# Re-ordering the loads, the start and the last row tile of a squared-ReLU MLP kernel

## The chip, the cores and the metric

The kernel runs on one core of a Trainium2 chip. The metric is device time in microseconds (us). Each profile belongs to one execution; each timing is a set of executions, compared with executions of the kernel before in the same rounds on the same chip.

The span in a profile is shorter than the timed figure of the same execution by 1.8 us (kernel before).

PE is TensorE (matmuls and transposes), ACT is ScalarE, DVE is VectorE, POOL is GpSimd, SP is SyncE, which only issues DMAs here (`nc.sync`). PE writes its results to PSUM; copying them from there to SBUF is called *evacuation*. A load *lands* when all its data has arrived. In a profile line, out<-in are the tiles written and read, L192 is a line of the kernel, xN a count, and [0.42 <-DVE xTw L132] means that the engine was idle for 0.42 us before, until DVE's line 132 had written xTw.

## The reference

```python
B, S, D, F = 1, 2048, 576, 4608          # all bf16
def reference(x, w1, b1, w2, b2):
    h = jnp.einsum("bsd,df->bsf", x, w1) + b1
    r = jnp.where(h > 0, h, 0)
    h = r * r
    return jnp.einsum("bsf,fd->bsd", h, w2) + b2
```

## The kernel before

The sequence is worked in four blocks of 512 rows. For each block, the *first product* (18 steps j) makes h transposed from w1 and x transposed; ACT applies bias and ReLU, DVE squares into hT. The *second product* (four row tiles of 128 rows) multiplies hT by w2. x has to be transposed on TensorE (PE): all of block 0 before anything else, the next block's rows inside the second product of the block before it ("mid transposes").

w1 is kept as two halves on partitions 0-63 and 64-127, which two 64-row matmuls read side by side; so x transposed is kept in windows shifted by 64. For block 0 all ten windows are transposed on PE (40 transposes for four row tiles); for blocks 1 to 3 only every second window is (20 transposes a block), and the others are copied from those by DMA.

```python
    load_x_block(0, (nc.sync, nc.scalar))      # two DMAs of 288 KB
    # ... 8 warm-up matmuls on zeros, identity ...
    nc.scalar.dma_start(out=b1_rows[0:NFT, :], in_=b1.rearrange("(ft p) -> ft p", p=P))
    nc.scalar.dma_start(out=b2_bc[:], in_=b2.partition_broadcast(P))
    j_chunks = [(0, 1), (1, 2), (2, 4), (4, 8), (8, 12), (12, 16), (16, 18)]
    for ci, (j0, j1) in enumerate(j_chunks):   # two DMAs (halves) per piece of w1
        ...
    load_x_block(1, (nc.sync, nc.sync))
    for c in range(NFT // W2CH):               # six pieces of w2, 864 KB each
        nc.sync.dma_start(out=w2_sb[:, c*W2CH:(c+1)*W2CH, :], in_=...)
    # PE: transpose b1_rows, then the 40 transposes of x block 0
    ...
    def phase_b(sb, hT, mid_tile=None):        # second product
        for jj in range(RT):
            for i, ft in enumerate(ft_order):  # ft_order = 0, 18, 1, 19, 2, 20, ...
                if mid_tile is not None and i == NFT // 2:
                    mid_tile(jj)               # mid transposes, in jj = 0 and 1
                for h in range(2):
                    nc.tensor.matmul(po[h][:, 0:DH], lhsT=hT[:, ft, ...], rhs=w2_sb[:, ft, ...], ...)
            for h in range(2):
                nc.vector.tensor_tensor(out=o_sb[...], in0=po[h][...], in1=b2_f[...], op=ALU.add)
            nc.sync.dma_start(out=out2[...], in_=o_sb[:])
```

The order of use in the second product: its second step (i = 1) reads ft 18, which lies in the fourth piece of w2, and i = 24 and i = 25 read the third and the sixth piece.

## Time and profile before

| | us |
|---|---|
| time, median of 13 runs (300.46 to 301.67) | 301.05 |
| span of the profiled execution (itself timed 301.67, the slowest of these 13) | 299.9 |
| first product of block 0 starts / lasts | 9.19 / 37.0 |
| first product of blocks 1 to 3 | 35.08 each |
| first matmul of the first second product to the start of the last matmul | 249.9 |
| end of the last matmul to the end of the span | 3.5 |

The page's part on the chain that ended last, followed back from the last instruction, by engine and then by line (shares of the span):

```profile
PE 92%; DMA 6%; SPq 0%; DVE 0%; DVEq 0%; issue 0%
PE po L192 47%; PE ph L171 35%; PE ph L173 10%; DMA w_h<-in_w_dram 6%; PE tp L143 1%; SPq L98 0%; DVE o_sb L201 0%; SPq L66 0%; DVEq L251 0%
```

PE is the bottleneck; nearly all that is not PE is a wait for w1 (named w_h). The same chain in order of time (start in us, length in us, what):

```profile
1.23 6.12 DMA w_h<-in_w_dram
...
8.01 10.81 DMA w_h<-in_w_dram
18.86 0.39 PE ph L173
...
46.23 4.52 PE po L192 x36
50.75 0.56 PE tp L143 x10
...
296.25 0.46 DVE o_sb L201
```

The chain hangs on w1 until 18.82 us, 9.6 us after the first product began; from 46.2 us on it is matmuls without a break. PE's own waits (engine, line, what it waited for: total us, times, longest):

```profile
PE ph L173 <- DMA w_h<-in_w_dram: 1.5, 1, 1.5
PE b1T_ps L156 <- DMA b_rows<-in_b_dram: 1.5, 1, 1.5
PE wps L79 <- DVE wz L75: 1.3, 1, 1.3
PE ph L171 <- DVE xTw L132: 0.4, 1, 0.4
```

So PE is held twice: once by the b1 rows ahead of the x transposes, once by a w1 piece inside the first product. The timeline of the two ends (start, length, engine, line, operation, out<-in, count):

```profile
1.25 3.58 PE L79 MATMUL wps<-wz 128*128 128x512 bf16 x8 [1.25 <-DVE wz L75]
6.37 2.39 PE L122 MATMUL tp<-ident,x_sb 128*128 128x128 bf16 x40
...
9.19 0.37 PE L171 MATMUL ph<-xTw,w_h 64*128 64x512 bf16 x1 [0.42 <-DVE xTw L132]
...
296.25 0.82 DVE L201 TENSOR_TENSOR o_sb<-po,b_f 128x288 bf16<-128x288 f32 x2 [8.00 <-PE po L192]
297.10 0.33 SPq L207 DMA_DIRECT2D out_dram<-o_sb  x1
```

### The profile page before, as it was taken

The page shows a single profiled execution, that of the slowest core. Times are in us where ns is not written, and L with a number is a line of the kernel's source. Part 1 is how long each engine was busy: PE and PEld are TensorE (multiplying, and loading weights), DVE is VectorE, ACT ScalarE, POOL GpSimd, SP SyncE. Part 2 cuts the span into 40 slices and gives each one's busy share as a digit, 9 for nine tenths or more (in the row PEclk, how much of TensorE's full clock was granted, in tenths as well). Part 3 has the DMA queues.
Part 4 walks back from the last instruction along what each step waited for, and adds up shares of the span by engine and source line. Part 5 has one row for each costly group of instructions (what it writes and reads, how often), then busy time and mean ns, then how long its engine had stood idle before and what let it go on. Part 6 is the DMA issues. An engine that isn't in the chain of part 4 may idle for free.

```text
span 299.9 us, 5764 instructions
## 1 busy us (share of the span) xinstructions
PE 291.6 (97%) x2557; PEld 182.6 (61%) x2557; DVE 77.0 (26%) x183; ACT 102.9 (34%) x162; POOL 3.0 (1%) x16
## 2 busy tenths in 40 slices
PE   6979999999999999999999999999999999999995
PEld 2534447787744445887764444778774444477773
DVE  1434442111034444001114444211003444400111
ACT  2656663010056666110016666401004666600000
POOL 2000000000000000000000000000000000000000
PEclk9999999999999999999999999999999999999999
DMA  7999996240000000212000000022000000000000
GB/s 179 201 203 207 320 357 214 61 138 2 21 22 0 2 0 2 39 30 50 22 20 2 1 2 0 2 61 42 20 20 22 0 2 0 2 0 23 20 23 20
DMA packets 21337, 17.63 MB, mean 59 GB/s; under 512 B 3264, under 2 KB 21312, under 8 KB 21312
## 3 DMA queue, kind: packets, MB, share of 16 engines
q1 hardware_dynamic: 20256, 16.67, 22.8%
q10 hardware_dynamic: 1056, 0.60, 0.8%
q8 instruction: 20, 0.33, 0.5%
q14 instruction: 5, 0.04, 0.0%
HBM read 13.13 MB, written 2.36 MB: 52 GB/s over the span
## 4 chain that ended last, share of the span: by engine, by line
PE 92%; DMA 6%; SPq 0%; DVE 0%; DVEq 0%; issue 0%
PE po L192 47%; PE ph L171 35%; PE ph L173 10%; DMA w_h<-in_w_dram 6%; PE tp L143 1%; SPq L98 0%; DVE o_sb L201 0%; SPq L66 0%; DVEq L251 0%
## 5 line engine op out<-in xcount | busy, mean ns | idle before, releaser
L192 PE MATMUL po<-w_sb,hT 128*128 128x288 bf16 x1152 | 142.8, 286 | 0.0
L173 PE MATMUL ph<-xTw,w_h 64*128 64x512 bf16 x648 | 140.7, 376 | 1.5 <-DMA w_h<-in_w_dram 1.5
L171 PE MATMUL ph<-xTw,w_h 64*128 64x512 bf16 x648 | 140.7, 376 | 0.4 <-DVE xTw L132 0.4
L177 ACT ACTIVATE r<-ph,b1T 128x512 bf16<-128x512 f32 x144 | 91.2, 684 | 118.6 <-PE ph L173 107.5
L192 PEld LDWEIGHTS <-hT 128*128 128x128 bf16 x1152 | 112.1, 98 | 29.6 <-DVE hT L178 1.7
L171 PEld LDWEIGHTS <-w_h 64*128 64x128 bf16 x648 | 60.6, 94 | 61.0 <-issue 0.7
L178 DVE TENSOR_TENSOR hT<-r 128x512 bf16<-128x512 bf16 x144 | 61.3, 426 | 85.6 <-ACT r L177 85.0
L173 PEld LDWEIGHTS <-w_h 64*128 64x128 bf16 x648 | 60.4, 94 | 17.3 <-DMA w_h<-in_w_dram 2.4
L201 DVE TENSOR_TENSOR o_sb<-po,b_f 128x288 bf16<-128x288 f32 x32 | 13.2, 453 | 127.9 <-PE po L192 127.9
L145 ACT COPY xTw<-tp 128x640 bf16<-128x640 bf16 x12 | 7.7, 695 | 35.1 <-PE tp L143 35.1
L79 PE MATMUL wps<-wz 128*128 128x512 bf16 x8 | 3.6, 627 | 1.3 <-DVE wz L75 1.3
L143 PE MATMUL tp<-ident,x_sb 128*128 128x128 bf16 x60 | 4.3, 219 | 0.0
L143 PEld LDWEIGHTS <-x_sb 128*128 128x128 bf16 x60 | 3.9, 98 | 0.3
L130 ACT COPY xTw<-tp 128x640 bf16<-128x640 bf16 x4 | 2.5, 706 | 4.4 <-PE tp L122 4.4
L79 PEld LDWEIGHTS <-wz 128*128 128x128 bf16 x8 | 1.0, 138 | 2.9 <-issue 1.7
L122 PE MATMUL tp<-ident,x_sb 128*128 128x128 bf16 x40 | 2.4, 219 | 0.0
L122 PEld LDWEIGHTS <-x_sb 128*128 128x128 bf16 x40 | 2.3, 98 | 0.0
L160 DVE CAST b_f<-b_bc 128x576 f32<-128x576 bf16 x1 | 0.5, 460 | 5.8 <-DMA b_bc<-in_b_dram 5.8
L62 POOL MEMSET x_sb<- 128x256 bf16 x4 | 1.2, 312 | 58.1 <-PE tp L143 51.4
L85 ACT ACT_TABLE_LOAD x1 | 1.3, 1283 | 1.3 <-PEq L240 1.3
L132 DVE COPY xTw<-tp 128x640 bf16<-128x640 bf16 x4 | 1.7, 481 | 0.0
L156 PE MATMUL b1T_ps<-ident,b_rows 128*128 128x128 bf16 x1 | 0.2, 216 | 1.5 <-DMA b_rows<-in_b_dram 1.5
(13 smaller groups left out, 3.3 us busy)
## 6 DMA issues: line engine op xcount, KB each, us to landing
w_sb<-in_w_dram SPq DMA_DIRECT2D x6, 864.0 KB, 11.5
w_h<-in_w_dram SPq DMA_DIRECT2D x6, 576.0 KB, 14.3
out_dram<-o_sb SPq DMA_DIRECT2D x16, 144.0 KB, 1.8
x_sb<-in_x_dram SPq DMA_DIRECT2D x7, 288.0 KB, 3.6
w_h<-in_w_dram SPq DMA_DIRECT2D x4, 288.0 KB, 10.3
xTw<-xTw SPq DMA_DIRECT2D x6, 160.0 KB, 2.6
xTw<-xTw SPq DMA_DIRECT2D x6, 128.0 KB, 2.4
w_h<-in_w_dram SPq DMA_DIRECT2D x3, 144.0 KB, 6.3
```

What stands on the lines that cost most here:

```text
L79: nc.tensor.matmul(wps[:], lhsT=wz[:, 0:P], rhs=wz[:, P:640], start=(i == 0), stop=(i == NWARM - 1))
L122: nc.tensor.transpose(tp[:, i, :], xs[:, j, w * H:w * H + P], ident[:])
L130: nc.scalar.copy(out=dst, in_=tp[:, :, :])
L132: nc.vector.tensor_copy(out=dst, in_=tp[:, :, :])
L143: nc.tensor.transpose(tp[:, n, :], xs[:, j, w * H:w * H + P], ident[:])
L145: nc.scalar.copy(out=xTw_v[:, :, 1, cols], in_=tp[:, :, :])
L171: nc.tensor.matmul(bx[:], lhsT=w1_h[0:H, c, j * P:(j + 1) * P], rhs=xTw[0:H, c + 1, scols], start=(c == 0), stop=(c == NC - 1))
L173: nc.tensor.matmul(by[:], lhsT=w1_h[H:P, c, j * P:(j + 1) * P], rhs=xTw[H:P, c, scols], start=(c == 0), stop=(c == NC - 1))
L177: nc.scalar.activation(out=r[:], in_=bank[:], func=ACT.Relu, bias=b1T[:, ft:ft + 1], scale=1.0)
L178: nc.vector.tensor_tensor(out=hT[:, ft, :], in0=r[:], in1=r[:], op=ALU.mult)
L192: nc.tensor.matmul(po[h][:, 0:DH], lhsT=hT[:, ft, jj * P:(jj + 1) * P], rhs=w2_sb[:, ft, h * DH:(h + 1) * DH], start=(i == 0), stop=(i == ...
L201: nc.vector.tensor_tensor(out=o_sb[:, h * DH:(h + 1) * DH], in0=po[h][:, 0:DH], in1=b2_f[:, h * DH:(h + 1) * DH], op=ALU.add,)
```

## The change

Its intent is to start PE earlier, keep it fed, and shorten the end. The core of the diff, cut:

```diff
-    load_x_block(0, (nc.sync, nc.scalar))
+    load_x_block(0, (nc.sync, nc.scalar, nc.sync, nc.scalar))     # four DMAs of 144 KB
-    NWARM = 8
+    NWARM = 5
-    nc.scalar.dma_start(out=b1_rows...)   # and b1 transposed before x
+    nc.gpsimd.dma_start(out=b1_rows...)   # and b1 transposed after x
-    j_chunks = [(0, 1), (1, 2), (2, 4), (4, 8), (8, 12), (12, 16), (16, 18)]
+    # (0,1) (1,2) (2,3) (3,4) (4,5) (5,6) (6,8) (8,10) (10,12) (12,15) (15,18), all on nc.sync
+    nc.sync.dma_start(out=b2_bc[:], ...)  # after w1; used as bf16, no cast
-    load_x_block(1, (nc.sync, nc.sync))   # ahead of w2
-    for c in range(NFT // W2CH):
+    for c in (0, 3, 1, 4, 2, 5):          # w2 in order of use
         nc.sync.dma_start(out=w2_sb[...], ...)
+    load_x_block(1, (nc.sync, nc.sync))   # after w2
-    hpool bufs=1, one xTw for all rows
+    hpool bufs=2, xTw per block, bufs=2
     def mid(jj):
-            if jj < 2:                    # row tiles 0 and 1
-                for j in (2 * jj, 2 * jj + 1): ...
-                dup_block(nsb, 2 * jj, 2, nc.sync)
+            if 1 <= jj < 3:               # row tiles 1 and 2
+                for j in (2 * jj - 2, 2 * jj - 1): ...
+                dup_block(nsb, 2 * jj - 2, 2, nc.gpsimd)
     # in phase_b:
+            if last and jj == RT - 1:     # last row tile: one half after the other,
+                for h in range(2):        # each with its own evacuation and store
+                    for i, ft in enumerate(ft_order):
+                        mmb(i, ft, h)
+                    evac(h)
+                    nc.sync.dma_start(out=out2[..., h * DH:(h + 1) * DH], in_=...)
...
```

Not in this cut: the loads of x blocks 2 and 3 stand after the second products of blocks 0 and 1 instead of ahead of them, ACT's table load comes later, and DVE makes both PSUM copies of the first row tile. The table load and the copies belong to the start.

More of the change, by code (lines that the diff above doesn't have):

```diff
@@ L39 @@
     NW = NC + 1
-    assert D % H == 0 and S % 512 == 0 and F % (2 * P) == 0
+    NH = NW // 2
+    assert D % H == 0 and S % 512 == 0 and F % (2 * P) == 0 and NW % 2 == 0
     SB = 512
@@ L48 @@
     wpool = ctx.enter_context(tc.tile_pool(name="wpool", bufs=1))
-    xpool = ctx.enter_context(tc.tile_pool(name="xpool", bufs=1))
+    xtpool = ctx.enter_context(tc.tile_pool(name="xtpool", bufs=2))
     xspool = ctx.enter_context(tc.tile_pool(name="xspool", bufs=2))
-    hpool = ctx.enter_context(tc.tile_pool(name="hpool", bufs=1))
+    hpool = ctx.enter_context(tc.tile_pool(name="hpool", bufs=2))
     rpool = ctx.enter_context(tc.tile_pool(name="rpool", bufs=4))
@@ L63, in load_x_block @@
         nc.gpsimd.memset(xs[:, :, H + D:XW], 0.0)
-        half = RT // 2
-        for i in range(2):
+        n = len(engs)
+        per = RT // n
+        for i in range(n):
             engs[i].dma_start(
-                out=xs[:, i * half:(i + 1) * half, H:H + D],
-                in_=x_view[:, sb * RT + i * half: sb * RT + (i + 1) * half, :],
+                out=xs[:, i * per:(i + 1) * per, H:H + D],
+                in_=x_view[:, sb * RT + i * per: sb * RT + (i + 1) * per, :],
             )
         x_stage[sb] = xs
-    load_x_block(0, (nc.sync, nc.scalar))
+    load_x_block(0, (nc.sync, nc.scalar, nc.sync, nc.scalar))
     wz = const.tile([P, 640], BF16, name="wz")
@@ L82, with load_w1 @@
     make_identity(nc, ident[:])
+    b1_rows = const.tile([P, P], BF16, name="b1_rows")
+    nc.gpsimd.memset(b1_rows[:], 0.0)
+    nc.gpsimd.dma_start(out=b1_rows[0:NFT, :], in_=b1.rearrange("(ft p) -> ft p", p=P))
+    w1_h = wpool.tile([P, NC, FH], BF16, name="w1_h")
+    w1_v = w1.rearrange("(c p) f -> p c f", p=H)
+    def load_w1(j0, j1):
+        for h in range(2):
+            nc.sync.dma_start(out=w1_h[h * H:(h + 1) * H, :, j0 * P:j1 * P],
+                              in_=w1_v[:, :, h * FH + j0 * P:h * FH + j1 * P])
+    NJ0 = 6
+    for (j0, j1) in [(0, 1), (1, 2), (2, 3), (3, 4), (4, 5), (5, 6)]:
+        load_w1(j0, j1)
+    for (j0, j1) in [(6, 8), (8, 10), (10, 12), (12, 15), (15, 18)]:
+        load_w1(j0, j1)
+    b2_bc = const.tile([P, D], BF16, name="b2_bc")
+    nc.sync.dma_start(out=b2_bc[:], in_=b2.partition_broadcast(P))
     warm = const.tile([P, 1], FP32, name="warm")
@@ L85 @@
     nc.scalar.activation(out=warm[:], in_=warm[:], func=ACT.Relu)
-    b1_rows = const.tile([P, P], BF16, name="b1_rows")
-    nc.gpsimd.memset(b1_rows[:], 0.0)
-    nc.scalar.dma_start(out=b1_rows[0:NFT, :], in_=b1.rearrange("(ft p) -> ft p", p=P))
-    b2_bc = const.tile([P, D], BF16, name="b2_bc")
-    nc.scalar.dma_start(out=b2_bc[:], in_=b2.partition_broadcast(P))
-    w1_h = wpool.tile([P, NC, FH], BF16, name="w1_h")
-    w1_v = w1.rearrange("(c p) f -> p c f", p=H)
-    j_chunks = [(0, 1), (1, 2), (2, 4), (4, 8), (8, 12), (12, 16), (16, 18)]
-    for ci, (j0, j1) in enumerate(j_chunks):
-        engs = (nc.sync, nc.scalar) if ci == 0 else (nc.sync, nc.sync)
-        engs[0].dma_start(out=w1_h[0:H, :, j0 * P:j1 * P], in_=w1_v[:, :, j0 * P:j1 * P])
-        engs[1].dma_start(out=w1_h[H:P, :, j0 * P:j1 * P], in_=w1_v[:, :, FH + j0 * P:FH + j1 * P])
-    load_x_block(1, (nc.sync, nc.sync))
     w2_sb = wpool.tile([P, NFT, D], BF16, name="w2_sb")
@@ L105, with alloc_xT @@
     W2CH = 6
-    for c in range(NFT // W2CH):
+    for c in (0, 3, 1, 4, 2, 5):
         nc.sync.dma_start(out=w2_sb[:, c * W2CH:(c + 1) * W2CH, :], in_=w2_view[:, c * W2CH:(c + 1) * W2CH, :])
-    xTw = xpool.tile([P, NW, S], BF16, name="xTw")
-    cp_flip = [0]
-    def transpose_rowtile(sb, j, tags, eng=None):
+    load_x_block(1, (nc.sync, nc.sync))
+    xT_blk = {}
+    def alloc_xT(sb):
+        xT_blk[sb] = xtpool.tile([P, NW, SB], BF16, name="xTw", tag="xTw")
+    last_act_copy = [None]
@@ L114, in transpose_rowtile, with copy_psum @@
+    def copy_psum(eng, dst, src):
+        if eng is nc.scalar:
+            last_act_copy[0] = nc.scalar.copy(out=dst, in_=src)
+        else:
+            nc.vector.tensor_copy(out=dst, in_=src)
+    def transpose_rowtile(sb, j, tags, engs):
         xs = x_stage[sb]
-        rt = sb * RT + j
-        cols = slice(rt * P, (rt + 1) * P)
+        cols = slice(j * P, (j + 1) * P)
         for hh in range(2):
             pool, tag = tags[hh]
-            tp = pool.tile([P, NW // 2, P], BF16, name="tp", tag=tag)
-            for i in range(NW // 2):
-                w = hh * (NW // 2) + i
+            tp = pool.tile([P, NH, P], BF16, name="tp", tag=tag)
+            for i in range(NH):
+                w = hh * NH + i
@@ L122, in transpose_rowtile @@
                 nc.tensor.transpose(tp[:, i, :], xs[:, j, w * H:w * H + P], ident[:])
-            if eng is None:
-                cp_flip[0] ^= 1
-                e = nc.vector if cp_flip[0] else nc.scalar
-            else:
-                e = eng
-            dst = xTw[:, hh * (NW // 2):(hh + 1) * (NW // 2), cols]
-            if e is nc.scalar:
-                nc.scalar.copy(out=dst, in_=tp[:, :, :])
-            else:
-                nc.vector.tensor_copy(out=dst, in_=tp[:, :, :])
-    xTw_v = xTw[:].rearrange("p (w t) s -> p w t s", t=2)
+            copy_psum(engs[hh], xT_blk[sb][:, hh * NH:(hh + 1) * NH, cols], tp[:, :, :])
@@ L136, in transpose_rowtile_nat @@
     def transpose_rowtile_nat(sb, j, pool, tag, eng):
         xs = x_stage[sb]
-        rt = sb * RT + j
-        cols = slice(rt * P, (rt + 1) * P)
-        tp = pool.tile([P, NW // 2, P], BF16, name="tp", tag=tag)
-        for n in range(NW // 2):
+        cols = slice(j * P, (j + 1) * P)
+        xv = xT_blk[sb][:].rearrange("p (w t) s -> p w t s", t=2)
+        tp = pool.tile([P, NH, P], BF16, name="tp", tag=tag)
+        for n in range(NH):
             w = 2 * n + 1
             nc.tensor.transpose(tp[:, n, :], xs[:, j, w * H:w * H + P], ident[:])
-        if eng is nc.scalar:
-            nc.scalar.copy(out=xTw_v[:, :, 1, cols], in_=tp[:, :, :])
-        else:
-            nc.vector.tensor_copy(out=xTw_v[:, :, 1, cols], in_=tp[:, :, :])
+        copy_psum(eng, xv[:, :, 1, cols], tp[:, :, :])
@@ L149, in dup_block @@
     def dup_block(sb, rt0, nrt, eng):
-        cols = slice((sb * RT + rt0) * P, (sb * RT + rt0 + nrt) * P)
-        nh = NW // 2
-        eng.dma_start(out=xTw_v[0:H, 1:nh, 0, cols], in_=xTw_v[H:P, 0:nh - 1, 1, cols])
-        eng.dma_start(out=xTw_v[H:P, 0:nh, 0, cols], in_=xTw_v[0:H, 0:nh, 1, cols])
+        cols = slice(rt0 * P, (rt0 + nrt) * P)
+        xv = xT_blk[sb][:].rearrange("p (w t) s -> p w t s", t=2)
+        eng.dma_start(out=xv[0:H, 1:NH, 0, cols], in_=xv[H:P, 0:NH - 1, 1, cols])
@@ L155 @@
+        eng.dma_start(out=xv[H:P, 0:NH, 0, cols], in_=xv[0:H, 0:NH, 1, cols])
+    alloc_xT(0)
+    for j in range(RT):
+        transpose_rowtile(0, j, [(ps_h, "ph"), (ps_o, "po")],
+                          engs=(nc.vector, nc.scalar) if j > 0 else (nc.vector, nc.vector))
     b1T_ps = ps_o.tile([P, P], BF16, name="b1T_ps", tag="po")
@@ L158, with a_step, alloc_hT @@
     nc.vector.tensor_copy(out=b1T[:], in_=b1T_ps[:, 0:NFT])
-    b2_f = const.tile([P, D], FP32, name="b2_f")
-    nc.vector.tensor_copy(out=b2_f[:], in_=b2_bc[:])
-    for j in range(RT):
-        transpose_rowtile(0, j, [(ps_h, "ph"), (ps_o, "po")])
-    def phase_a(sb, hT):
-        scols = slice(sb * SB, (sb + 1) * SB)
-        for j in range(NJ):
-            bx = ps_h.tile([P, SB], FP32, name="ph", tag="ph")
-            by = ps_h.tile([P, SB], FP32, name="ph", tag="ph")
-            for c in range(NC):
-                nc.tensor.matmul(bx[:], lhsT=w1_h[0:H, c, j * P:(j + 1) * P], rhs=xTw[0:H, c + 1, scols],
-                                 start=(c == 0), stop=(c == NC - 1))
-                nc.tensor.matmul(by[:], lhsT=w1_h[H:P, c, j * P:(j + 1) * P], rhs=xTw[H:P, c, scols],
-                                 start=(c == 0), stop=(c == NC - 1))
-            for bank, ft in ((bx, j), (by, NJ + j)):
-                r = rpool.tile([P, SB], BF16, name="r", tag="r")
-                nc.scalar.activation(out=r[:], in_=bank[:], func=ACT.Relu, bias=b1T[:, ft:ft + 1], scale=1.0)
-                nc.vector.tensor_tensor(out=hT[:, ft, :], in0=r[:], in1=r[:], op=ALU.mult)
+    hTs = {}
+    def a_step(sb, j):
+        xT = xT_blk[sb]
+        hT = hTs[sb]
+        bx = ps_h.tile([P, SB], FP32, name="ph", tag="ph")
+        by = ps_h.tile([P, SB], FP32, name="ph", tag="ph")
+        for c in range(NC):
+            nc.tensor.matmul(bx[:], lhsT=w1_h[0:H, c, j * P:(j + 1) * P], rhs=xT[0:H, c + 1, :],
+                             start=(c == 0), stop=(c == NC - 1))
+            nc.tensor.matmul(by[:], lhsT=w1_h[H:P, c, j * P:(j + 1) * P], rhs=xT[H:P, c, :],
+                             start=(c == 0), stop=(c == NC - 1))
+        for bank, ft in ((bx, j), (by, NJ + j)):
+            r = rpool.tile([P, SB], BF16, name="r", tag="r")
+            nc.scalar.activation(out=r[:], in_=bank[:], func=ACT.Relu, bias=b1T[:, ft:ft + 1], scale=1.0)
+            nc.vector.tensor_tensor(out=hT[:, ft, :], in0=r[:], in1=r[:], op=ALU.mult)
+    def alloc_hT(sb):
+        hTs[sb] = hpool.tile([P, NFT, SB], BF16, name="hT", tag="hT")
     ft_order = []
@@ L182, with phase_b @@
         ft_order += [j, NJ + j]
-    def phase_b(sb, hT, mid_tile=None):
+    def phase_b(sb, hT, mid_tile=None, last=False):
         for jj in range(RT):
@@ L187, in phase_b, with mmb, evac @@
             po = [ps_o.tile([P, 512], FP32, name="po", tag="po") for _ in range(2)]
+            o_sb = opool.tile([P, D], BF16, name="o_sb", tag="o_sb")
+            def mmb(i, ft, h):
+                nc.tensor.matmul(
+                    po[h][:, 0:DH],
+                    lhsT=hT[:, ft, jj * P:(jj + 1) * P],
+                    rhs=w2_sb[:, ft, h * DH:(h + 1) * DH],
+                    start=(i == 0),
+                    stop=(i == NFT - 1),
+                )
+            def evac(h):
+                nc.vector.tensor_tensor(
+                    out=o_sb[:, h * DH:(h + 1) * DH],
+                    in0=po[h][:, 0:DH],
+                    in1=b2_bc[:, h * DH:(h + 1) * DH],
+                    op=ALU.add,
+                )
+            if last and jj == RT - 1:
+                for h in range(2):
+                    for i, ft in enumerate(ft_order):
+                        mmb(i, ft, h)
+                    evac(h)
+                    nc.sync.dma_start(out=out2[rt * P:(rt + 1) * P, h * DH:(h + 1) * DH], in_=o_sb[:, h * DH:(h + 1) * DH])
+                continue
             for i, ft in enumerate(ft_order):
@@ L191, in phase_b @@
                 for h in range(2):
-                    nc.tensor.matmul(
-                        po[h][:, 0:DH],
-                        lhsT=hT[:, ft, jj * P:(jj + 1) * P],
-                        rhs=w2_sb[:, ft, h * DH:(h + 1) * DH],
-                        start=(i == 0),
-                        stop=(i == NFT - 1),
-                    )
-            o_sb = opool.tile([P, D], BF16, name="o_sb", tag="o_sb")
-            for h in range(2):
-                nc.vector.tensor_tensor(
-                    out=o_sb[:, h * DH:(h + 1) * DH],
-                    in0=po[h][:, 0:DH],
-                    in1=b2_f[:, h * DH:(h + 1) * DH],
-                    op=ALU.add,
-                )
+                    mmb(i, ft, h)
+            for h in range(2):
+                evac(h)
             nc.sync.dma_start(out=out2[rt * P:(rt + 1) * P, :], in_=o_sb[:])
@@ L210, in mid @@
         def mid(jj):
-            if jj < 2:
-                for j in (2 * jj, 2 * jj + 1):
+            if jj == 1:
+                alloc_xT(nsb)
+            if 1 <= jj < 3:
+                for j in (2 * jj - 2, 2 * jj - 1):
                     transpose_rowtile_nat(nsb, j, ps_h, "ph", nc.scalar)
-                dup_block(nsb, 2 * jj, 2, nc.sync)
+                dup_block(nsb, 2 * jj - 2, 2, nc.gpsimd)
         return mid
-    for sb in range(NSB):
-        hT = hpool.tile([P, NFT, SB], BF16, name="hT", tag="hT")
-        phase_a(sb, hT)
-        if sb + 1 < NSB:
-            if sb + 2 < NSB:
-                load_x_block(sb + 2, (nc.sync, nc.sync))
-            phase_b(sb, hT, mid_tile=make_mid(sb + 1))
-        else:
-            phase_b(sb, hT)
+    alloc_hT(0)
+    for j in range(NJ):
+        a_step(0, j)
+    phase_b(0, hTs[0], mid_tile=make_mid(1))
+    load_x_block(2, (nc.sync, nc.sync))
+    alloc_hT(1)
+    for j in range(NJ):
+        a_step(1, j)
+    phase_b(1, hTs[1], mid_tile=make_mid(2))
+    load_x_block(3, (nc.sync, nc.sync))
+    alloc_hT(2)
+    for j in range(NJ):
+        a_step(2, j)
+    phase_b(2, hTs[2], mid_tile=make_mid(3))
+    alloc_hT(3)
+    for j in range(NJ):
+        a_step(3, j)
+    phase_b(3, hTs[3], last=True)
 _INS = ['x', 'w1', 'b1', 'w2', 'b2']
```

## The prediction

> **What bounds the kernel now.** TensorE. The page gives PE 97% busy of a 299.9 us span, and the chain of waits is 92% PE and 6% DMA. The timeline shows a repeating block: the first product of a 512-row block takes 35.08 us (82.73 to 117.81), the second 35.28 us, the ten-transpose groups for the next block 1.12 us. From the start of the first second-product (46.23) to the last matmul (about 296.3) there is no gap: 250.1 us. So only the two ends can be shortened.
>
> - Head: the first product starts at 9.19 and ends at 46.23, 37.04 us against 35.08 undisturbed. The missing 2.0 us are mainly one stall, about 17 to 18.9 us, on a w1 chunk of four column tiles (the chain of waits has DMA w1 as the releaser until 18.82).
> - Before 9.19: warm-up matmuls until 4.8, then PE waits 1.49 us for the b1 rows (waits view) because the b1 transpose stands ahead of the x transposes; x had landed by 4.71. Forty transposes take 2.39 us, PSUM copies end near 9.1.
> - Tail: from the last matmul to the span's end 3.6 us, of it two evacuations in a row (0.82 us) and a 144 KB store.
>
> **What the change does.**
> 1. x block 0 in four DMAs ahead of all else, b1 on another queue and transposed after x, b2 late and never cast: transposes can start near 3.5-4 us instead of 6.3. They are then paced by copies (DVE 0.48 us x5, ACT 0.70 us x3 plus waits). I expect the first product to start near 7.4: about 1.8 us gained. The first w1 tile must land by then; moving queues gives no bandwidth (the Trainium skill, "DMA: Bandwidth & Descriptors", Issuing engines are not separate DMA queues). In this trace w1 moves at about 200 GB/s, whatever the chunk size: 295 KB per column tile in 1.45 us, against 1.95 us that PE needs for it. I estimate the first tile at about 6.9.
> 2. w1 in one-tile pieces at first: since supply (1.45 us) is quicker than use (1.95 us) only granularity caused the stall. It should vanish: 2.0 us gained.
> 3. w2 order, double-buffered hT and per-block xT, mid transposes later, copies of xT on the GpSimd queue: all off the path. PE shows no wait there now, and the copies still have about 14 us until use (2.6 us to landing now). Gain 0, loss 0.
> 4. Last row tile split by halves: one evacuation (about 0.4 us) and half the store leave the tail: 0.5 us gained.
> 5. Three warm-up matmuls fewer. The skill's "TensorE: Matmul & The Clock Gate" (Part 1, The HAM clock gate) says roughly 3.4 us of activity bring the full clock. The trace agrees: warm-up matmuls start 0.43 us apart[...]. Five give only 2.1 us, so transposes, perhaps first matmuls, may run at half rate. I allow 0 to 2 us, about 0.3 us expected.
>
> Sum: -1.8 - 2.0 - 0.5 + 0.3, about -4.1 us: **297.0 us**, range 295.4 to 299.5. Faster by over 2% (below 295.1) 7%, within 2% 91.5%, slower 1.5%.
>
> **What would show it.** First-product start near 7.4 and lasting 35.1 us (timeline); no PE wait on w1 after the first tile (waits); 250 us from there to the end unchanged; last evacuation 0.4 us before the last store[...].
>
> **What would make it wrong.** Half-rate clock persisting into the first product (+1 to +2 us); b1 arriving late by the GpSimd queue and holding PE at its transpose; first w1 tile late because one of the 16 landings trails the others; the GpSimd-issued xT copies landing after the next block's first product starts (a wait at three boundaries).

## The result, and the profile after

The changed kernel took 297.67 us in the median (296.95 to 298.11, 8 runs) against 301.05 us: ratio 0.9886, interval [0.9873, 0.9899]. That is 3.4 us. The change is clear of noise but within 2%.

The chain that ended last, by engine and by line:

```profile
PE 98%; DVE 0%; issue 0%
PE po L198 48%; PE ph L175 46%; PE ph L177 2%; PE tp L148 1%; PE tp L138 1%; PE wps L81 1%; DVE xTw L128 0%; DVE o_sb L207 0%; DVE wz L77 0%
```

No DMA is left in it. In order of time:

```profile
1.26 2.31 PE wps L81 x5
3.63 3.02 PE tp L138 x35
6.68 0.50 DVE xTw L128
7.22 0.37 PE ph L175
...
42.36 13.34 PE po L198 x108
55.70 0.56 PE tp L148 x10
...
292.51 0.46 DVE o_sb L207
```

PE's waits, all of them:

```profile
PE wps L81 <- DVE wz L77: 1.3, 1, 1.3
PE ph L175 <- DVE xTw L128: 0.2, 1, 0.2
```

And the timeline of the two ends:

```profile
3.63 3.29 PE L138 MATMUL tp<-ident,x_sb 128*128 128x128 bf16 x40
...
292.51 0.46 DVE L207 TENSOR_TENSOR o_sb<-po,b_bc 128x288 bf16<-128x288 f32 x1 [3.95 <-PE po L198]
292.99 0.33 SPq L219 DMA_DIRECT2D out_dram<-o_sb  x1
```

The first product starts at 7.22 instead of 9.19, lasts 35.07 instead of 36.97, the 249.9 us in the middle are the same to 0.01, and the tail is 3.01 instead of 3.54. Together 1.97 + 1.90 + 0.53 = 4.4 us of span.

Why 4.4 in the profiles and 3.4 in the times? The profiled execution of the kernel before was 0.62 us slower than its median, that of the changed kernel 0.29 us faster than its own, and the time outside the span is 0.11 us longer in the changed kernel. 4.4 - 0.6 - 0.3 - 0.1 = 3.4. One trace of a kernel whose runs spread over 1.2 us is not its median; the pair of traces flatters the change.

### The profile page after: what moved, and what is told of

Read it like the earlier page. It is cut to its first block, busy times and chain, and to the rows that moved or that the text cites. A ratio compares the mean times of both kernels' runs of the same rounds, so it can differ in the third digit from the quotient of the medians.

```text
span 295.5 us, 5772 instructions
## 1 busy us (share of the span) xinstructions
PE 290.9 (98%) x2554; PEld 185.0 (63%) x2554; DVE 77.5 (26%) x183; ACT 102.3 (35%) x161; POOL 11.5 (4%) x29
## 4 chain that ended last, share of the span: by engine, by line
PE 98%; DVE 0%; issue 0%
PE po L198 48%; PE ph L175 46%; PE ph L177 2%; PE tp L148 1%; PE tp L138 1%; PE wps L81 1%; DVE xTw L128 0%; DVE o_sb L207 0%; DVE wz L77 0%
## 5 line engine op out<-in xcount | busy, mean ns | idle before, releaser
L207 DVE TENSOR_TENSOR o_sb<-po,b_bc 128x288 bf16<-128x288 f32 x32 | 13.3, 453 | 127.3 <-PE po L198 127.3
L126 ACT COPY xTw<-tp 128x640 bf16<-128x640 bf16 x15 | 9.6, 696 | 64.0 <-PE tp L148 61.3
L154 POOL DMA_DIRECT2D xTw<-xTw x6 | 3.8, 628 | 188.7 <-ACT xTw L126 188.7
L148 PE MATMUL tp<-ident,x_sb 128*128 128x128 bf16 x60 | 4.3, 219 | 0.0
L155 POOL DMA_DIRECT2D xTw<-xTw x6 | 4.1, 676 | 0.0
L148 PEld LDWEIGHTS <-x_sb 128*128 128x128 bf16 x60 | 3.9, 98 | 0.3
L138 PEld LDWEIGHTS <-x_sb 128*128 128x128 bf16 x40 | 3.1, 120 | 0.9 <-POOL x_sb L64 0.9
L81 PE MATMUL wps<-wz 128*128 128x512 bf16 x5 | 2.3, 628 | 1.3 <-DVE wz L77 1.3
L128 DVE COPY xTw<-tp 128x640 bf16<-128x640 bf16 x5 | 2.5, 492 | 3.5 <-PE tp L138 3.4
L138 PE MATMUL tp<-ident,x_sb 128*128 128x128 bf16 x40 | 3.3, 259 | 0.1
L63 POOL MEMSET x_sb<- 128x256 bf16 x4 | 1.3, 319 | 10.9 <-issue 6.8
L64 POOL MEMSET x_sb<- 128x256 bf16 x4 | 1.3, 319 | 0.0
```

Of the source, the lines that this page charges most:

```text
L81: nc.tensor.matmul(wps[:], lhsT=wz[:, 0:P], rhs=wz[:, P:640], start=(i == 0), stop=(i == NWARM - 1))
L126: last_act_copy[0] = nc.scalar.copy(out=dst, in_=src)
L138: nc.tensor.transpose(tp[:, i, :], xs[:, j, w * H:w * H + P], ident[:])
L148: nc.tensor.transpose(tp[:, n, :], xs[:, j, w * H:w * H + P], ident[:])
L154: eng.dma_start(out=xv[0:H, 1:NH, 0, cols], in_=xv[H:P, 0:NH - 1, 1, cols])
L155: eng.dma_start(out=xv[H:P, 0:NH, 0, cols], in_=xv[0:H, 0:NH, 1, cols])
```

## The experiments

The profile pair suggests a plain sum: an earlier start, no stall, a shorter tail, and the rest (w2 order, x block 1 last, later mid transposes, double buffering) worth nothing. I call that **theory A**. **Theory B**: the loads are one stream whose pieces arrive at fixed times, and each piece has a deadline; removing PE's wait on one piece only moves PE up to the next. Then the parts do not add, and the "worthless" ones protect the gain. All timings below are medians in us, each with that of the kernel before in the same rounds. All outputs are right. Where I set a run against the changed kernel (297.67), the two come from different rounds; the medians of the kernel before go from 300.90 to 301.19 over all rounds, so such a difference carries some 0.3 us beside the noise.

| run | this | before | ratio, 95% interval |
|---|---|---|---|
| tail_only | 300.87 | 300.90 | 1.0001 [0.9974, 1.0028] |
| w1_pieces_only | 300.64 | 300.90 | 0.9993 [0.9971, 1.0015] |
| head_only | 300.30 | 300.90 | 0.9977 [0.9957, 0.9998] |
| w1_pieces_w2_order | 301.23 | 300.95 | 1.0014 [0.9997, 1.0030] |
| stream_only | 299.67 | 301.13 | 0.9960 [0.9942, 0.9977] |
| after_warm8 | 297.98 | 300.90 | 0.9908 [0.9882, 0.9934] |
| after_w1_coarse | 299.19 | 300.95 | 0.9948 [0.9935, 0.9961] |
| after_w2_plain_order | 300.62 | 300.95 | 0.9985 [0.9960, 1.0010] |
| after_steady_undone | 300.80 | 300.95 | 0.9997 [0.9963, 1.0030] |
| after_hT1_sp | 297.97 | 301.13 | 0.9896 [0.9878, 0.9914] |
| dma_transpose | 294.59 | 301.13 | 0.9785 [0.9770, 0.9801] |
| dma_transpose_w1_two_queues | 294.41 | 301.19 | 0.9776 [0.9756, 0.9796] |

### One part alone, on the kernel before

**tail_only** is the kernel before with only the `if last and jj == RT - 1` branch of the diff.

> The kernel before with only the last row tile split by halves. Theory (the two ends are all there is): 0.4 to 0.6 us faster than before, with one evacuation and a 72 KB store after the last matmul. Rival (the tail is paced by the latency of the last store, not by evacuation or size): at most 0.2 us.

Its timeline at the end:

```profile
296.03 0.46 DVE L200 TENSOR_TENSOR o_sb<-po,b_f 128x288 bf16<-128x288 f32 x1 [3.95 <-PE po L191]
296.51 0.33 SPq L212 DMA_DIRECT2D out_dram<-o_sb  x1
```

One evacuation instead of two follows the last matmul, and the tail is 3.18 us in its trace. The timing cannot resolve it: the interval of 0.27% either way is 0.8 us. Across traces, tails without the split are 3.5 to 3.7 us (3.54 before, 3.53 in w1_pieces_only, 3.73 in head_only), with it 3.0 to 3.5 us (3.01 in the changed kernel, 3.44 in dma_transpose). The part is worth about 0.4 us by the traces, and the timing alone leaves it open.

**w1_pieces_only** replaces one line.

```diff
-    j_chunks = [(0, 1), (1, 2), (2, 4), (4, 8), (8, 12), (12, 16), (16, 18)]
+    j_chunks = [(0, 1), (1, 2), (2, 3), (3, 4), (4, 5), (5, 6), (6, 8), (8, 10), (10, 12), (12, 15), (15, 18)]
```

> The kernel before with only the w1 pieces of the changed kernel (one tile at a time at first). Theory (granularity causes the stall at 17 to 19 us): the first product lasts about 35.1 us instead of 37.0 and the run is 1.5 to 2 us faster. Rival (the w1 supply rate is short, or more DMA issues cost as much): the stall is spread over several waits and the gain is under 0.7 us.

The first product lasted 35.07 us, so granularity did cause the stall. But the time hardly moved (ratio 0.9993). PE's waits show what took its place:

```profile
PE po L192 <- DMA w_sb<-in_w_dram: 0.5, 1, 0.5
```

The second product now starts at 44.47 instead of 46.16 and stops at its second step for the fourth w2 piece (w_sb), which the trace's landing records put at 45.3 us. Both expectations missed: the stall was not spread and the pieces cost nothing; the gain was passed on to another load. In the kernel before, that piece landed at 45.1, about 1.3 us before its use (two matmuls after 46.16): that is all the gain there was room for.

**head_only** is the earlier start alone: x in four DMAs, b1 on the GpSimd queue and transposed after x, b2 late, all w1 pieces on SP, five warm-ups, ACT table warmed later.

> The kernel before with the earlier start alone: x in four pieces, b1 on the GpSimd queue and transposed after x, b2 late, five warm-up matmuls; w1 pieces as before, tail as before. Theory A (the parts of the prediction add up): first product starts about 1.8 us earlier and the run is 1.5 to 1.8 us faster. Theory B (the end of the first product is set by the absolute arrival of the four-tile w1 pieces): it starts about 1.8 us earlier, waits longer for the same pieces, and the run gains less than 0.7 us.

The first product began at 7.83 (the clock was late in this run, see below) and still stalled (no matmul starts between 15.60 and 17.09 us); it lasted 36.56 us. The waits view names ACT for it:

```profile
PE ph L174 <- ACT r L178: 1.1, 1, 1.1
```

This is a tie broken the wrong way: that ReLU ended at 17.05, and the second half of the four-tile w1 piece landed at 17.05 too, and the matmul that resumed at 17.09 is the first to read it. The time fell by 0.6 us by the medians (ratio 0.9977, so 0.1 to 1.3 us). It lies between the theories: the start gained well over a microsecond, but the stall stayed, although the piece itself came earlier (17.05 instead of 18.82, with the first w1 tile complete at 6.8 instead of 8.9), which theory B as I wrote it had not allowed for.

The three parts alone sum to about 0.9 us by the medians, each uncertain by 0.6 to 0.8 us; all changes together give 3.4.

### One part taken back, on the changed kernel

**after_w1_coarse** has the pieces of before.

```diff
-    # (0,1) (1,2) (2,3) ... (15,18)
+    for (j0, j1) in [(0, 1), (1, 2), (2, 4), (4, 8), (8, 12), (12, 16), (16, 18)]:
         load_w1(j0, j1)
```

> The changed kernel with the coarse w1 pieces of before. Theory B (absolute arrival): first product starts at 7.2 as in the changed kernel but waits on the first four-tile piece until 17.0 to 18.9 us; first product 36.5 to 38.5 us, run 1.4 to 3.0 us slower than the changed kernel. Rival (parts add up, stall worth what it was before): 1.4 us slower, first product 36.5 us.

```profile
PE ph L174 <- DMA w_h<-in_w_dram: 1.6, 1, 1.6
```

The piece arrived at 16.7 us, PE waited, and the first product lasted 37.35 us. The run is 1.5 us slower than the changed kernel (299.19 against 297.67), at the low end of what theory B expected and close to theory A's number as well: this run does not tell them apart.

**after_w2_plain_order** takes back two lines that the prediction had called worthless.

```diff
-    for c in (0, 3, 1, 4, 2, 5):
+    for c in range(NFT // W2CH):
 # and load_x_block(1, ...) ahead of this loop again
```

> The changed kernel with the w2 pieces back in natural order and x block 1 again ahead of w2. Theory B (arrival deadlines: with natural order the fourth w2 piece, which the second matmul pair of the second product needs, landed at 45.3 us in w1_pieces_only): the second product starts at 42.3 but is held until about 45.5, and the run is 2.5 to 3.2 us slower than the changed kernel, nearly all its gain gone. Rival (the recorded prediction's step 3: w2 order is off the path): 0 to 0.3 us slower.

```profile
PE po L199 <- DMA w_sb<-in_w_dram: 0.7, 1, 0.7
```

300.62 us: 2.95 us slower than the changed kernel, within theory B's expectation, and nearly the whole gain. The trace shows the wait, but only about 1 us of it (matmul starts 42.62 and 43.59, the piece landing at 43.55), and the profiled execution was the fastest of six: 298.41 us, the others 300.23 to 301.19. The other five have no trace. That they lose more on the same load is inferred, not shown: with w1, x block 1 and w2 in this same order the piece landed at 45.3 in w1_pieces_only, which by my estimate would hold PE for 2.6 us here (use due at 42.7).

**after_steady_undone** takes back three things at once that are "steady state".

```diff
-    hpool bufs=2
+    hpool bufs=1
-            if 1 <= jj < 3: ... dup_block(nsb, 2 * jj - 2, 2, nc.gpsimd)
+            if jj < 2: ...      dup_block(nsb, 2 * jj, 2, nc.sync)
```

> The changed kernel with single-buffered hT, the mid transposes back in row tiles 0 and 1 and the xT copies back on the SP queue. Theory (off the path, as predicted): same as the changed kernel within 0.4 us, and from the second product's first matmul to the last matmul 249.9 us again. Rival (double buffering contributes): over 0.5 us slower, with that stretch longer than 249.9 us.

300.80 us, and 251.2 us instead of 249.9 in the middle. My theory for this run fell, but the trace names neither buffer nor queue:

```profile
PE tp L148 <- DMA x_sb<-in_x_dram: 1.2, 1, 1.2
```

The mid transposes, back in row tile 0, are due after the matmul of 46.3 us, begin at 47.8, and wait for x block 1, which in the new order of loads is last (in the changed kernel's trace its first half, which these transposes need, lands at 47.2). Again the profiled execution was the fastest (298.71; the others 299.69 to 302.29). The three slowest, 301.66 to 302.29, are also the ones with a mean granted clock of 0.992 to 0.994 where the others show 0.998 to 1.000. A mean of 0.994 over a span of 299.8 us is about 3.6 us at half clock (an estimate), or 1.8 us lost, near what separates these three from the other two untraced ones. Whether the wait brought it about is not shown: no trace of such a run exists, and in the traced one the clock stayed full through the wait of 1.2 us.

**after_hT1_sp** separates the three: single hT and SP queue as above, but the mid transposes left in row tiles 1 and 2.

> The changed kernel with single-buffered hT and the xT copies back on the SP queue, but the mid transposes left in row tiles 1 and 2. Theory (of after_steady_undone only the early mid transposes cost, because they wait for x block 1, which now comes last): same as the changed kernel, 297.2 to 298.2 us, no gap after the first product. Rival (double buffering or the GpSimd queue contributes): over 0.8 us slower.

297.97 us (297.67 to 298.28), as the theory expected. So the buffers and the queue are worth nothing that these runs resolve (the interval is 0.5 us either way), and the place of the mid transposes is what cost about 3 us in after_steady_undone. The one wait in its trace after the start is again the stream:

```profile
PE po L198 <- DMA w_sb<-in_w_dram: 0.4, 1, 0.4
```

This is the sixth w2 piece, which landed at 48.8 in this run and at 46.4 in the changed kernel's trace, against a use at about 48.2 to 48.4 (50 matmuls of 0.1225 us after the second product's start). Pieces move by 2.4 us from run to run, so even the changed kernel has little to spare.

### The stream as one change

**w1_pieces_w2_order** adds to w1_pieces_only the w2 order and x block 1 last, but not the later mid transposes.

```diff
 # on top of w1_pieces_only
-    load_x_block(1, ...)                  # ahead of w2
-    for c in range(NFT // W2CH):
+    for c in (0, 3, 1, 4, 2, 5):
+    load_x_block(1, ...)                  # after w2
```

> The kernel before with fine w1 pieces and also the changed w2 order, x block 1 after w2. Theory B: first product 35.1 us, no wait on w2, so the gain that w1_pieces_only lost comes out: 1.0 to 1.8 us faster than before, start still at about 9.3. Rival (fine pieces cost something else): no better than w1_pieces_only, within 0.5 us of before.

```profile
PE tp L143 <- DMA x_sb<-in_x_dram: 1.8, 1, 1.8
```

301.23 us, no gain: my expectation failed. The w2 wait is gone and its place is taken by x block 1, which the mid transposes in row tile 0 need. I had overlooked that the two edits belong together; after_steady_undone shows the same wait from the other side.

**stream_only** adds the later mid transposes as well.

```diff
 # on top of w1_pieces_w2_order
-            if jj < 2:        # mid transposes in row tiles 0 and 1
+            if 1 <= jj < 3:   # in row tiles 1 and 2
```

> The kernel before with the three parts that belong to one load stream: fine w1 pieces, w2 pieces in order of use with x block 1 last, mid transposes in row tiles 1 and 2. Start, tail, buffers as before. Theory (each part alone only passes the wait on to the next load; together they remove it): first product 35.1 us, then 249.9 us without a gap, 1.3 to 1.9 us faster than before. Rival (something else in the fine pieces costs): within 0.6 us of before.

299.67 us, 1.5 us faster than before (ratio 0.9960). From the first second product on there are 249.9 us without a gap, and PE waits for no weight. With start and tail still as before, this is the size of the stall as the median run has it, less than the 1.9 us of the one trace of before. (Its own profiled execution was an odd one, 301.03 against 299.44 to 299.93 for the other five: the clock again, below.)

So fine pieces alone give 0.3 us by the medians, fine pieces with the w2 order -0.3, and with the later mid transposes 1.5. The start and the tail (with the buffers and the queue) then add 2.0 more (299.67 to 297.67), though head_only and tail_only gave 0.6 and 0.0.

### Warm-ups and the clock

**after_warm8** sets `NWARM = 8` in the changed kernel.

> The changed kernel with eight warm-up matmuls instead of five. Theory (three cold warm-up matmuls stand in front of the x transposes, 0.43 us each, but the full clock comes at about the same time): transposes start at 4.8 instead of 3.6, run mostly at full rate, and the first product starts 0.2 to 0.8 us later; run 0.1 to 0.8 us slower than the changed kernel. Rival (five are too few to bring the clock): 0.3 us or more faster than the changed kernel.

297.98 us, 0.3 us above the changed kernel of another batch: the same within what these runs resolve (half-width of the interval 0.26%, or 0.8 us). The trace shows why:

```profile
1.26 3.48 PE L81 MATMUL wps<-wz 128*128 128x512 bf16 x8 [1.26 <-DVE wz L77]
4.57 2.40 PE L138 MATMUL tp<-ident,x_sb 128*128 128x128 bf16 x40
```

The transposes start 0.94 us later than with five warm-ups but take 2.40 instead of 3.29 us, because the full clock is already there. The last transpose starts at 6.75 and 6.70 us.

The moment of the full clock differs from run to run. The record of the granted clock in each trace gives it for the eight traces with five warm-ups, next to the start of the first product:

| trace | full clock from, us | first product starts, us |
|---|---|---|
| after_w1_coarse | 4.43 | 6.69 |
| after_steady_undone | 4.87 | 6.94 |
| after_hT1_sp | 5.15 | 7.02 |
| changed kernel | 5.54 | 7.22 |
| dma_transpose_w1_two_queues | 5.60 | 7.29 |
| after_w2_plain_order | 6.04 | 7.41 |
| dma_transpose | 6.98 | 7.87 |
| head_only | 7.01 | 7.83 |

Up to 1.2 us of start hang on it, and the runs of the changed kernel spread over 1.16 us. A single trace says little about the start. Eight warm-ups are no insurance: in stream_only's trace PE ran eight, then paused for the b1 rows, and the full clock came at 10.70 us:

```profile
1.25 3.59 PE L79 MATMUL wps<-wz 128*128 128x512 bf16 x8 [1.25 <-DVE wz L75]
5.60 0.26 PE L156 MATMUL b1T_ps<-ident,b_rows 128*128 128x128 bf16 x1 [0.76 <-DMA b_rows<-in_b_dram]
5.66 4.47 PE L122 MATMUL tp<-ident,x_sb 128*128 128x128 bf16 x40
```

All forty transposes ran at half rate (4.47 us against 2.40).

### A version that beats both

Between the two ends PE has no gap, so only work taken off PE still shortens the run. **dma_transpose** removes the 60 mid transposes and the loads that fed them. Each transposing load takes 128 of the 576 columns, so the last one overlaps the one before it: it takes window 8 (columns 448 to 575) and window 9 is copied from it.

```diff
-    load_x_block(1, ...); load_x_block(2, ...); load_x_block(3, ...)
             if jj == 1:
                 alloc_xT(nsb)
-            if 1 <= jj < 3: ... transpose_rowtile_nat(...); dup_block(...)
+                for w in (1, 3, 5, 7, 8):
+                    nc.sync.dma_start(out=xT_blk[nsb][:, w, :],
+                                      in_=x2[rows, (w - 1) * H:(w - 1) * H + P], transpose=True)
+                nc.gpsimd.dma_start(out=xv[0:H, 1:NH - 1, 0, :], in_=xv[H:P, 0:NH - 2, 1, :])
+                nc.gpsimd.dma_start(out=xv[H:P, 0:NH - 1, 0, :], in_=xv[0:H, 0:NH - 1, 1, :])
+                nc.gpsimd.dma_start(out=xT_blk[nsb][0:H, NW - 1, :], in_=xT_blk[nsb][H:P, NW - 2, :])
```

> The changed kernel with the 60 TensorE transposes of blocks 1 to 3 replaced by transposing loads of x on the SP queue. Theory (TensorE has no gap between the two ends, so only work taken off TensorE still shortens it; three groups of 1.12 us are 3.4 us): 294.0 to 294.8 us, 246.5 us from the second product to the last matmul. Rival (the transposing loads are slow and land after the next block needs them, or disturb the other loads): a wait at three block boundaries, no gain or slower.

294.59 us: ratio 0.9785 to the kernel before, and 3.1 us below the changed kernel. The middle is 246.54 us, 3.35 less, where three groups of 1.12 are 3.36. The chain in order of time runs straight through the second product:

```profile
43.01 35.39 PE po L197 x288
78.39 0.32 PE ph L174
```

and the view of DMA issues (out<-in, engine, count, KB, median us to landing) show the transposing loads landing 3.6 us after issue in the median (those for block 1 are all in by 52.7 us and their copies by 58.3, for a use at 78.4):

```profile
xTw<-in_x_dram SPq DMA_TRANSPOSE x15, 3.6
```

**dma_transpose_w1_two_queues** asks a side question: w1 moves at 194 to 224 GB/s (changed kernel, windows between 6 and 26 us) and w2 at 357 (32 to 46 us).

```diff
         for h in range(2):
-            nc.sync.dma_start(out=w1_h[h * H:(h + 1) * H, ...
+            eng = nc.scalar if (h == 1 and j0 < 3) else nc.sync
+            eng.dma_start(out=w1_h[h * H:(h + 1) * H, ...
```

> dma_transpose with the second half (partitions 64 to 127) of the first three w1 tiles issued from the ACT queue, so that transfers into both partition halves are in flight together. Question: why w1 moves at about 200 GB/s and w2 at about 355. If the limit is that one transfer writes only 64 partitions at a time, the third w1 tile has fully landed by about 7.6 us. If the two transfers simply share the engines (the Trainium skill says transfers to disjoint partition halves serialize), it lands at 9.2 us or later as in the run before (9.59 us). Time in either case within 0.5 us of dma_transpose (294.6 us), because the first product's start is set by transposes and copies, not by w1.

The third w1 tile landed at 9.75 us, not earlier than 9.59. Both queues moved packets at the same time (between 7 and 8 us 81 KB by SP's and 112 KB by ACT's), but the sum, 193 GB/s, is hardly more than the 189 that SP's queue moved alone in dma_transpose: transfers to the two partition halves shared one rate. This agrees with the Trainium skill, "DMA: Bandwidth & Descriptors", Rules for kernel authors, which says that they serialize. What makes w1's rate little more than half of w2's, no run here isolates (a w1 transfer writes 64 partitions, a w2 transfer 128). The time, 294.41 us, is that of dma_transpose within the intervals.

## Why the prediction was right or wrong

The total was right: 297.67 us against 297.0 predicted, in the range, and within 2% as thought likely; 3.4 us of gain against 4.1.

- *Start, "near 7.4, about 1.8 us gained"*: 7.22 in the trace, 1.97 gained. Right. Over eight traces it lies between 6.69 and 7.87.
- *Stall, "2.0 us gained"*: the mechanism was right (one-tile pieces remove it, 35.07 us), the size was read from one trace. That trace shows 1.9 us, tail_only's 1.4, and stream_only's timing gives 1.5. This is the mis-sized term: about 0.5 of the missing 0.7 us. The rest (0.2, or 0.5 with the warm-up term below at zero) lies within the spread of the start.
- *Tail, "0.5 us gained"*: 0.53 in the pair of traces and about 0.4 over all traces, right; the timing of tail_only could not show it.
- *Five warm-ups, "about 0.3 us expected"*: eight are no faster (297.98). In the trace of before, 512-column matmuls start 0.43 us apart among the warm-ups and 0.216 us apart in the first product; in the changed kernel's, 0.216 from the first product's beginning. The cost of half-rate transposes is paid back by the earlier start, so the term should have been zero, with a spread of 1.2 us around it.
- *Step 3, "w2 order, ... mid transposes later, ...: all off the path. PE shows no wait there now ... Gain 0, loss 0"*: this step failed. Taking back the w2 order costs 2.95 us, taking back the later mid transposes (with buffers and queue, which after_hT1_sp clears) 3.1 us. PE showed no wait there because it was late: the fourth w2 piece landed 1.3 us before its use, and the change brings PE forward by nearly four. Much of these two losses falls in runs without a trace; the traced runs, the fastest of each six, show 0.8 and 1.3 us of it, on w2 and on x block 1. The sum came out right only because these edits, counted as nothing, were in the change and kept both waits out of it; as far as this step goes that was luck. Double buffering and the GpSimd queue were judged rightly.

Theory B is what the runs support, with one correction from head_only: the arrival times are not quite fixed, since an earlier start of the stream moves them too. Open remain the untraced slow runs of after_w2_plain_order and after_steady_undone, and, in these runs, the reason for w1's rate.

## What to carry to other kernels

"PE does not wait there" is a statement about PE's present position. Before you count the gain of bringing an engine forward by some microseconds, list for each later load when it lands and when it is first used; each gap smaller than the gain is the next stall, and edits that only move such loads are part of the gain. Test parts both ways, alone and taken back: parts that give nothing alone may each carry nearly all of it.

## What the Trainium skill lacked or had wrong

- "TensorE: Matmul & The Clock Gate", Part 4 (PE-mode transpose) says that the full clock does not engage for transposes because they don't count as busy the same way. In head_only and dma_transpose PE ran nothing but transposes from 3.5 us on, and the full clock came at 7.01 and 6.98 us, 3.4 us after the last warm-up matmul had ended (3.57 us); the transposes, 0.107 us apart until then, follow 0.056 us apart. The profile lists them as MATMUL; whether they use the mode that the page speaks of, no trace shows.
- The same page, Part 1, puts the change of clock about 4 us into the activity, within 500 ns from run to run. Here the first matmul is always at 1.25 to 1.26 us, and the full clock came between 4.01 us (w1_pieces_only) and 7.01 us (head_only), so 2.8 to 5.8 us into it, and once at 10.70 us (stream_only, with a pause of 0.8 us). The free-running window that the page describes fits a spread of this kind; the 500 ns do not.
